# Reciprocals of the softmax moved to POOL in odd slots, and two more items of 36 turned by squares, in a top-k attention and GELU kernel

## The chip, the cores and the metric

The kernel runs on one core of a Trainium2 chip. The metric is the device time of one execution in microseconds, the median of several runs. The core's engines work side by side, each through its own instructions in order: PE (matmuls, and transposes as matmuls), DVE (searches for the largest values, block transposes), ACT (exponentials, GELU, copies out of PE's accumulators), POOL (small sums and products) and SP, which here issues DMAs. An instruction starts when those before it on its engine allow it and the semaphores it waits for have come.

## What is computed

```python
B, H, S, D = q.shape                      # 8, 8, 576, 64; top_k = 32
scores = scale * np.matmul(q, k.transpose(0, 1, 3, 2))
kth = np.partition(scores, -top_k, axis=-1)[..., -top_k:-top_k + 1]
scores = np.where(scores >= kth, scores, -1000000000.0)
scores = scores - np.max(scores, axis=-1, keepdims=True)
attn = np.exp(scores)
attn = attn / (np.sum(attn, axis=-1, keepdims=True) + 1e-09)
x = np.matmul(attn, v)                    # then (B,H,S,D) -> (B*S, H*D)
h = x @ w_in                              # 4608 x 512 times 512 x 2048
out = (0.5 * h * (1.0 + erf(h / sqrt(2)))) @ w_out
```

The division by the sum is what the change is about: each row of 576 exponentials is multiplied with 1 / (sum + 1e-9).

## The kernel before

The attention is cut into 144 items. An item is 128 query rows of two heads side by side, so its tile `s` has 128 partitions and 2 x 576 columns. 36 items (`RINGS`) belong to two batches and are called a ring here; slot or item m of 36 means its number modulo 36. The main loop goes over slots n = 0 to 147, and in slot n every stage works at an item of its own: PE makes the scores of item n+2, DVE searches item n, ACT selects and exponentiates item n-1, POOL normalises item n-1, item n-2 is turned, and the product with v is made for the pair of items that ends in n-3. The flag `few` is set from slot 13 on; the statements below that ask for it hold from there. Pieces of the MLP (`h_ps`, `y_ps`) are dealt out over the slots on PE, and what is left of them follows after the last search. The order of the instructions on each engine is the order in which this Python code issues them.

One slot, as far as the change touches it:

- DVE, `top_k` (L487): four rounds, each with two MAX8 (L513, one for each head), the first three with two MATCH_REPLACE8 behind (L516). The first two rounds go over 288 values each, the element-wise larger of the two halves of a row (`larger`, L442); the last two go over all 576. Between round two and three stands `middle()`, which is `square_p` of item n-2 (L610, the block transpose L614), if that item goes by squares. After the last MAX8 comes `last()`: in slots with `few` it issues `larger` of item n+2 and then `inverse` of item n-1, the reciprocal L534. `larger` is also called at the start of every slot for item n+1, where it does nothing if that has been done.
- POOL: `smaller` of item n+1 (L485), `add_small` of item n-1 (L540, adds 1e-9 to the sums), then, behind the search's end, `threshold` of item n (L527 the negative of the 32nd value, L528 the exponent's bias), `normalise` of item n-1 (L582, the product of the whole tile with the reciprocals), `sum_up` of item n+2 (L477), and small sums of the MLP's second matmul from a list.
- ACT: `select` of item n-1 (L547, waits for L527), and the exponential (L559), which leaves the sum of its row in `den`. Among these stand GELUs and copies out of the accumulators.
- An item is turned in one of two ways. By PE: nine transposes (L666 and eight of L680), which ACT copies to `pt` (L669, L695). Or by squares: DVE turns blocks of 32 x 32 in place, four DMAs write the tile to DRAM (`write_p`, L616) and four read it back into `pt` (`read_p`, L626), all on SP's queue. `squared` (L586) says which: from item 27 on most even items, the last items of a batch, and those odd ones for which `moved` holds.
- `moved(i)` (L596) holds for items 36 to 135 with i modulo 36 in `LATER`. A moved item's product with v is made one slot later than otherwise: in slot n, `mid = [n - 4]` is then attended in the middle of the slot, and only behind it is the next item's tile read. `room_in` (L1141) gives PE two MLP pieces more in the slot whose product is put off, and two fewer in the one before.

The tile `stat` holds, for each item and both heads, `neg`, `bias`, `den` and `rden`, two columns each. Of `s` there are seven buffers, of `lists` and `stat` two, of `pt` one.

Of the kernel before, what the change touches and what calls it, by code (L numbers as in the profile page):

```python
# [8 lines left out]
TOPK = 32  # L9
# [5 lines left out]
def kernel(  # L15
# [19 lines left out]
    nc = tc.nc  # L35
    f32, i32, u32 = mybir.dt.float32, mybir.dt.int32, mybir.dt.uint32
    bf16, i16, u16 = mybir.dt.bfloat16, mybir.dt.int16, mybir.dt.uint16
    AF = mybir.ActivationFunctionType
    ALU = mybir.AluOpType

    B, H, S, D = q.shape
    P = 128
# [19 lines left out]
    const = ctx.enter_context(tc.tile_pool(name="const", bufs=1))  # L62
# [47 lines left out]
    def flush():  # L110
        held[0] = False
        while late_issues:
            late_issues.pop(0)()
        late_issues.extend(later)
        later.clear()
# [61 lines left out]
    DIAGS = START - 1  # L177
    SINGLE = range(18, 28)
    words = {}
    bounds = const.tile([P, 2], f32, name="bounds")  # L180
    low, high = bounds[:, 0:1], bounds[:, 1:2]
    nc.gpsimd.memset(low, -EXP0 * 2.0**20)
    nc.gpsimd.memset(high, EXP0 * 2.0**-40)

# [85 lines left out]
    N = len(items)  # L272
# [4 lines left out]
    few = [False]  # L277
# [55 lines left out]
    S_of, stat_of = {}, {}  # L333
# [98 lines left out]
    def paired(i):  # L432

        return PAIRED <= i < N and i not in SINGLE
# [7 lines left out]
    def larger(i):  # L442

        if paired(i) and i not in have_larger:
            have_larger.add(i)
            nc.vector.tensor_tensor(lists_for(i)[:, :, 0], *halves_of(i), op=ALU.max)  # L446

    def into_of(i):

        if i < 2 and i not in into_lists:  # L450
            into_lists[i] = work.tile([P, 2, 2, HS], f32, tag="pt", bufs=1, name="into")
        return into_lists.get(i, lists_of[i])
# [28 lines left out]
    def smaller(i):  # L481

        if paired(i):
            both, top = lists_of[i][:, :, 1].bitcast(i32), lists_of[i][:, :, 0].bitcast(i32)
            nc.gpsimd.tensor_tensor(into_of(i)[:, :, 1].bitcast(i32), both, top, op=ALU.subtract)  # L485

    def top_k(i, last, middle):  # L487


        stat_of[i] = st = {  # L490
            "first": work.tile([P, 2, 8], f32, tag="first", name="first"),
        }
        stat = work.tile([P, 4, 2], f32, tag="stat", name="stat")
        st.update((n, stat[:, x]) for x, n in enumerate(("neg", "bias", "den", "rden")))
        top = work.tile([P, 2, 16], f32, tag="top", bufs=1, name="top")
        into = [st["first"]] + [
            top[:, :, 8:16] if r == TOPK // 8 - 1 else top[:, :, 0:8] for r in range(1, TOPK // 8)
        ]
        if paired(i):
            t = lists_of[i]  # L500
            u = into_of(i)
            both = u.rearrange("p e h n -> p e (h n)")
            rounds = [(t[:, :, 0], u[:, :, 0]), (u[:, :, 0], u[:, :, 0])]
            rounds = [(*(rounds[r] if 16 * r < TOPK else (both, both)), x) for r, x in enumerate(into)]
        else:
            s = S_of[i].rearrange("p (e n) -> p e n", e=2)
            t = work.tile([P, 2, S], f32, tag="lists", name="rest")
            rounds = [(s if r == 0 else t, t, x) for r, x in enumerate(into)]
        for r, (src, dst, x) in enumerate(rounds):
            if 16 * r == TOPK:  # L510
                middle()
            for e in range(2):
                nc.vector.max(x[:, e], src[:, e])  # L513
            if r < len(rounds) - 1:
                for e in range(2):
                    nc.vector.match_replace(dst[:, e], x[:, e], src[:, e], LOWEST)  # L516
            if r == len(rounds) - 1:
                last()

        st["kth"] = top[:, :, 15]  # L520

    def threshold(i):

        if i < 0 or i >= N:
            return
        st = stat_of[i]
        nc.gpsimd.tensor_scalar(st["neg"], st["kth"], -1.0, None, op0=ALU.mult)  # L527
        nc.gpsimd.tensor_tensor(st["bias"], st["kth"], st["first"][:, :, 0], op=ALU.subtract)  # L528

    def inverse(i):  # L530
        if i < 0 or i >= N:
            return
        st = stat_of[i]
        nc.vector.reciprocal(st["rden"], st["den"])  # L534

    def add_small(i):
        if i < 0 or i >= N:
            return
        st = stat_of[i]
        nc.gpsimd.tensor_scalar(st["den"], st["den"], 1e-9, None, op0=ALU.add)  # L540
# [50 lines left out]
            return i % RINGS != RINGS // 2 - 1  # L591
        return moved(i) or (i % 2 == 0 and i % RINGS != 12)

    LATER = (3, 13, 25, 31)

    def moved(i):  # L596

        return RINGS <= i < N - 8 and i % RINGS in LATER

# [7 lines left out]
    RINGS = 2 * len(items) // B  # L607
    turned = {}

    def square_p(i):  # L610

        if squared(i):
            s = S_of[i]
            nc.vector.transpose(s, s)  # L614

    def write_p(i):  # L616

        if squared(i):
            turned[i] = d = dram.tile([SQ, NJ + NM, P // SQ, P], f32, tag="turned", name="turned")
            s = S_of.pop(i).rearrange("p (x j) -> p x j", j=SQ)  # L620
            d = d.rearrange("i c k n -> i (c k) n")
            for a in range(P // SQ):
                rows = slice(a * SQ, (a + 1) * SQ)
                nc.sync.dma_start(out=d[:, :, rows], in_=s[rows])
# [498 lines left out]
    def mlp(n):  # L1123
        for _ in range(n):
            if done[0] >= len(pieces) or pieces[done[0]][0] > ready[0] or left[0] == 0:
                return
            pieces[done[0]][1]()
            done[0] += 1
            left[0] -= 1
            if eager[0]:  # L1130
                run_gelus()
                run_small(9)
# [72 lines left out]
    for n in range(ahead):  # L1205
# [87 lines left out]
        if few[0]:  # L1293
            room = ODD if n % 2 else 0
            if mid and (mid[0] in starts_next or mid[0] % RINGS == LATER[0]):
                mlp(1)
# [34 lines left out]
            softmax(n - 1, 1)  # L1331
        if n > 0:
            smaller(n + 1)
        add_small(n - 1)
        for piece in tr[-1:] + prep:
            piece(None)
            mlp(1)
# [6 lines left out]
        run_gelus()  # L1344
        if n < N:
            def last():
                if few[0]:
                    larger(n + 2)
                inverse(n - 1)

            top_k(n, last, lambda: square_p(n - 2))
            write_p(n - 2)
            flush()
            if n == 0:
                larger(1)
        else:
            inverse(n - 1)
        threshold(n)
        if n == 0:
            smaller(1)  # L1360
        normalise(n - 1)
# [59 lines left out]
```

## Time and profile before

| what | us |
|---|---|
| median of 3 runs | 1461.71 (1461.59 to 1461.82) |
| profiled execution | 1461.3 |
| its span on the core | 1459.5 |
| last search's end, from the span's start | 1375.3 |

The granted clock of PE was 1.0 over the run. Times in the lines below are microseconds from the span's start unless marked ns. In a timeline row the first number is the start, the second the duration (of a merged row the time from the first start to the last end), then engine, line and operation, what it writes and reads with sizes, how many, and in brackets how long the engine had been idle before it and what ended that. A row of a group has the busy time and the mean duration in ns, then the idle time just before such instructions. A row of the view of waits has the total wait, how often, and names the waiting instruction first and what it waited for behind the arrow. An instruction on DVE or POOL can start some 0.06 to 0.08 us before the one ahead of it ends, so costs are taken from start to start.

### The profile page before, as it was taken

How to read it: one execution, taken by the hardware profiler on the slowest of the kernel's cores; microseconds unless marked ns; L12 is line 12 of the kernel's file. 1: busy time of each engine (PE TensorE's matmuls, PEld its weight loads, DVE VectorE, ACT ScalarE, POOL GpSimd, SP SyncE). 2: the span in 40 equal slices, each digit the busy share in tenths (PEclk: the TensorE clock that was granted, in tenths of full speed). 3: DMA queues.
4: the chain of work that ended last, by engine and by line, in shares of the span. 5: the costliest groups of instructions: out<-in, count | busy, mean ns of one | idle time of the engine just before them, and what ended most of it. 6: DMA issues, size and time to landing. Idle time of an engine off the chain costs nothing.

```text
span 1459.5 us, 26550 instructions
## 1 busy us (share of the span) xinstructions
PE 1442.6 (99%) x8621; PEld 1123.9 (77%) x8621; DVE 1329.6 (91%) x3339; ACT 1056.4 (72%) x1883; POOL 1128.4 (77%) x1290
## 2 busy tenths in 40 slices
PE   8999999999999999999999999999999999999999
PEld 6776678877777777787777778787777777787887
DVE  7999999999999999999999999999999999999601
ACT  7999977777777777767777777777676767677620
POOL 6877657877798878878888878887788887878632
PEclk9999999999999999999999999999999999999999
DMA  7524310045454446456554365456554444543200
GB/s 196 150 87 126 84 48 1 9 98 104 90 113 89 87 87 142 82 113 128 111 99 96 65 117 116 90 112 127 117 102 106 90 80 84 127 98 85 53 15 15
DMA packets 591819, 136.49 MB, mean 94 GB/s; under 512 B 504352, under 2 KB 583232, under 8 KB 591680
## 3 DMA queue, kind: packets, MB, share of 16 engines
q1 hardware_dynamic: 590416, 134.37, 43.5%
q8 instruction: 68, 1.11, 0.3%
q14 instruction: 71, 0.58, 0.1%
q10 hardware_dynamic: 1200, 0.39, 0.1%
q0 software_dynamic: 64, 0.03, 0.0%
HBM read 85.19 MB, written 49.55 MB: 92 GB/s over the span
## 4 chain that ended last, share of the span: by engine, by line
PE 44%; POOL 11%; DVE 7%; issue 3%; ACT 3%; DMA 1%; SPq 0%; DVEq 0%; POOLq 0%; ACTq 0%
PE h_ps L820 17%; PE y_ps L976 11%; PE o L751 5%; PE s_ps L408 3%; POOL s L582 3%; DVE top L513 3%; DVE lists L516 2%; POOL lists L485 2%; POOL lists L477 2%; PE seven L974 2%; PE tp L680 2%; PE y_ps L938 2%; PE y_ps L941 1%; DMA turned<-s 1%; DVE s L614 1%
## 5 line engine op out<-in xcount | busy, mean ns | idle before, releaser
L820 PE MATMUL h_ps<-xT,w_in_sb 128*128 128x256 f32 (+1 forms) x2560 | 533.0, 361 | 0.0
L820 PEld LDWEIGHTS h_ps<-xT,w_in_sb 128*128 128x128 f32 x2560 | 438.9, 191 | 69.2 <-issue 10.9
L513 DVE MAX8 top<-lists 128x8 f32<-128x576 f32 (+1 forms) x792 | 475.9, 641 | 0.0
L547 ACT ACTIVATE s<-s,stat 128x576 f32<-128x576 f32 x288 | 219.2, 786 | 123.0 <-POOL stat L527 122.9
L516 DVE MATCH_REPLACE8 lists<-top,lists 128x288 f32<-128x288 f32 (+1 forms) x528 | 308.0, 589 | 0.0
L582 POOL TENSOR_TENSOR s<-s,stat 128x1152 f32<-128x1152 f32 x135 | 284.8, 2109 | 10.1 <-DVE stat L534 5.3
L559 ACT ACTIVATE s<-s,stat 128x576 f32<-128x576 f32 x288 | 225.2, 787 | 7.6
L485 POOL TENSOR_TENSOR lists<-lists 128x576 int32<-128x576 int32 x132 | 186.6, 1413 | 3.1
L477 POOL TENSOR_TENSOR lists<-s 128x576 int32<-128x576 int32 x133 | 188.2, 1415 | 0.0
L540 POOL TENSOR_SCALAR stat<-stat 128x2 f32<-128x2 f32 x144 | 44.4, 309 | 163.0 <-ACT s L559 156.1
L751 PE MATMUL o<-pt,raw_v 128*64 128x256 f32 x1280 | 152.9, 384 | 1.0 <-ACT pt L685 0.4
L416 ACT ACTIVATE s<-s_ps 128x1024 f32<-128x1024 f32 x127 | 126.4, 1046 | 35.2 <-PE s_ps L408 35.0
L751 PEld LDWEIGHTS o<-pt,raw_v 128*64 128x64 f32 x1280 | 86.8, 136 | 80.9 <-issue 38.1
L976 PE MATMUL y_ps<-w_out_sb,sum 128*128 128x256 f32 x472 | 140.4, 379 | 0.0
L408 PE MATMUL s_ps<-kt,qm 64*128 64x512 f32 x512 | 131.2, 621 | 1.1 <-ACT s L414 0.8
L836 ACT ACTIVATE g<-h_ps 128x512 f32<-128x512 f32 x144 | 78.2, 595 | 66.6 <-PE h_ps L820 66.0
L446 DVE TENSOR_TENSOR lists<-s 128x576 f32<-128x576 f32 x133 | 106.2, 799 | 17.8 <-ACT s L381 5.8
L976 PE MATMUL y_ps<-w_out_sb,g 128*128 128x256 f32 x480 | 116.4, 382 | 0.0
L516 DVE MATCH_REPLACE8 lists<-first,lists 128x288 f32<-128x288 f32 x264 | 114.4, 439 | 0.0
L513 DVE MAX8 first<-lists 128x8 f32<-128x288 f32 x268 | 105.8, 434 | 0.0
L976 PEld LDWEIGHTS y_ps<-w_out_sb,g 128*128 128x128 f32 x480 | 90.4, 190 | 15.0 <-issue 3.1
L976 PEld LDWEIGHTS y_ps<-w_out_sb,sum 128*128 128x128 f32 x472 | 89.8, 190 | 12.1
(162 smaller groups left out, 2359.0 us busy)
## 6 DMA issues: line engine op xcount, KB each, us to landing
turned<-s SPq DMA_DIRECT2D x272, 144.0 KB, 3.6
pt<-turned SPq DMA_DIRECT2D x272, 144.0 KB, 3.2
raw_v<-in_v_dram SPq DMA_DIRECT2D x64, 128.0 KB, 2.5
raw_q<-in_q_dram SPq DMA_DIRECT2D x112, 72.0 KB, 2.3
raw_k<-in_k_dram SPq DMA_DIRECT2D x112, 72.0 KB, 2.4
out_dram<-y SPq DMA_DIRECT2D x30, 256.0 KB, 3.1
w_out_sb<-in_moe_w_in_dram SPq DMA_DIRECT2D x14, 511.8 KB, 4.9
w_out_sb<-in_moe_w_out_dram SPq DMA_DIRECT2D x10, 511.8 KB, 4.1
```

The source lines that it names most:

```text
L408: nc.tensor.matmul(s_ps[:, e], lhsT=q_t[rows, :], rhs=kt[rows, main_keys(pair)], start=True, stop=True)
L416: nc.scalar.activation(spread(s, S + TL, SM), s_ps, func=AF.Copy, scale=scale)
L477: nc.gpsimd.tensor_tensor(t[:, :, 1].bitcast(i32), a.bitcast(i32), b.bitcast(i32), op=ALU.add)
L485: nc.gpsimd.tensor_tensor(into_of(i)[:, :, 1].bitcast(i32), both, top, op=ALU.subtract)
L513: nc.vector.max(x[:, e], src[:, e])
L516: nc.vector.match_replace(dst[:, e], x[:, e], src[:, e], LOWEST)
L547: nc.scalar.activation(s, s, func=AF.Prelu, bias=st["neg"][:, e : e + 1], scale=1.0, alpha=STEEP)
L559: nc.scalar.activation(s, s, func=AF.Exp, bias=st["bias"][:, e : e + 1], scale=1.0, accum_out=st["den"][:, e : e + 1],)
L582: nc.gpsimd.tensor_tensor(s, s, wide, op=ALU.mult)
L751: nc.tensor.matmul(o[e * D : (e + 1) * D, 0:n], lhsT=vt[:, j, e, :], rhs=pt[:, e * NJ + j if j < NM else NM, :], start=(j == 0), stop=(j = ...
L820: nc.tensor.matmul(h_tile(u)[:, i, :], lhsT=w_in_sb[:, ko, f * P : (f + 1) * P], rhs=xT[:, ko, c0 : c0 + n], start=(ko == 0), stop=(ko == ...
L976: nc.tensor.matmul(acc[names][:, k], lhsT=lhsT, rhs=rhs, start=(j == 0 and k == 0), stop=(j == FT // 2 - 1 and k == 1),)
```

## The change

Four things are done at once. A column of -1 is put beside the two bounds. In slots with `few` and odd n (`by_power`), `add_small` of item n-1 moves from before the transposes' tail to behind `threshold` of item n, and the reciprocal is made by POOL, as the sum to the power -1, right behind it; DVE's reciprocal falls away there. In even slots DVE keeps the reciprocal, but `larger` of item n+2 is no longer issued ahead of it, save in slot 34 of 36: it follows at the start of the next slot. In even slots with `few` the square of item n-2 is issued behind the two MAX8 of the third round and no longer ahead of them. And `LATER` has 5 and 23 as well: items 41, 59, 77, 95, 113 and 131 go by squares.

```diff
-    bounds = const.tile([P, 2], f32, name="bounds")
+    bounds = const.tile([P, 3], f32, name="bounds")
+    minus = bounds[:, 2:3]
...
+    nc.gpsimd.memset(minus, -1.0)
...
-            if 16 * r == TOPK:
+            if 16 * r == TOPK and not (few[0] and i % 2 == 0):
                 middle()
             for e in range(2):
                 nc.vector.max(x[:, e], src[:, e])
+            if 16 * r == TOPK and few[0] and i % 2 == 0:
+                middle()
...
+    def power(i):
+        st = stat_of[i]
+        nc.gpsimd.tensor_tensor(
+            st["rden"], st["den"],
+            bass.AP(tensor=minus.tensor, offset=minus.offset, ap=[list(minus.ap[0]), [0, 2]]),
+            op=ALU.pow,
+        )
...
-    LATER = (3, 13, 25, 31)
+    LATER = (3, 5, 13, 23, 25, 31)
...
-        add_small(n - 1)
+        by_power = few[0] and n % 2 and n < N
+        if not by_power:
+            add_small(n - 1)
...
             def last():
-                if few[0]:
+                if few[0] and n % RINGS == RINGS - 2:
                     larger(n + 2)
-                inverse(n - 1)
+                if not by_power:
+                    inverse(n - 1)
...
         threshold(n)
+        if by_power:
+            add_small(n - 1)
+            power(n - 1)
         if n == 0:
             smaller(1)
         normalise(n - 1)
```

## The prediction

> **What bounds the kernel now.** I read the busy times first, then the same by stage (one ring, 36 slots, from 704 to 1046 us, and what follows the last search), then who waited for whom, then the timeline around two kinds of slot.
>
> ```profile
> PE 1442.6 (99%) x8621; PEld 1123.9 (77%) x8621; DVE 1329.6 (91%) x3339; ACT 1056.4 (72%) x1883; POOL 1128.4 (77%) x1290
> ...
> 704.40:1046.40 342.00, 341.01 (x2014) 265.91 (x2013) 333.01 (x838) 249.08 (x450) 283.56 (x322) 1.00 0.52 105
> ...
> 1375.30:1459.50 84.20, 80.36 (x402) 68.66 (x399) 5.07 (x13) 18.20 (x39) 28.06 (x39) 0.99 0.04 13
> ```
>
> Columns of the last two: span, then busy us (instructions) of PE, its weight loads, DVE, ACT, POOL. In a ring DVE is idle 9.0 of 342.0 us and PE 1.0. Both look full, but PE's ends are modelled. The tail of 84.2 us is MLP work on PE alone, so a slot that gets longer before it moves the end by as much.
>
> The Trainium skill ("Trainium Kernel Development and Optimization", Performance Expectations) calls matmul busy time a bad metric and the share of weight loads a good one. By that share the ring (265.91 of 342.0, 78%) runs at 95% of the tail's rate (68.66 of 84.2, 82%), so that PE has some 16 us to spare in a ring; by the busy row 1.0. The first would leave more room for DVE to be the pace, the second less.
>
> ```profile
> POOL stat L540 <- ACT s L559: 156.1, 65, 5.7
> ACT s L547 <- POOL stat L527: 122.9, 45, 6.2
> ...
> DVE stat L534 <- POOL stat L540: 27.8, 27, 6.2
> ```
>
> Columns: total us, times, the longest. DVE's one large wait is the reciprocal behind POOL's add: 27.8 us in 27 of 144 slots, and that is the whole of what taking it away can give back on DVE. POOL waits 156.1 us for exponentials, ACT 122.9 us for thresholds. First, an ordinary pair, odd slot 75 and even slot 76:
>
> ```profile
> 730.83 1.41 DVE L513 MAX8 top<-lists 128x8 f32<-128x576 f32 x2
> 732.35 0.78 DVE L446 TENSOR_TENSOR lists<-s 128x576 f32<-128x576 f32 x1
> 733.04 0.15 DVE L534 RECIPROCAL stat<-stat 128x2 f32<-128x2 f32 x1
> 733.12 0.79 DVE L513 MAX8 first<-lists 128x8 f32<-128x288 f32 x2
> ...
> 740.29 1.40 DVE L513 MAX8 top<-lists 128x8 f32<-128x576 f32 x2
> 741.80 0.76 DVE L446 TENSOR_TENSOR lists<-s 128x576 f32<-128x576 f32 x1
> 742.48 0.15 DVE L534 RECIPROCAL stat<-stat 128x2 f32<-128x2 f32 x1
> 742.56 0.79 DVE L513 MAX8 first<-lists 128x8 f32<-128x288 f32 x2
> ```
> ```profile
> 731.43 0.22 POOL L540 TENSOR_SCALAR stat<-stat 128x2 f32<-128x2 f32 x1 [2.10 <-ACT s L559]
> 732.33 0.22 POOL L527 TENSOR_SCALAR stat<-top 128x2 f32<-128x2 f32 x1 [0.67 <-DMA raw_q<-in_q_dram]
> 732.50 0.67 POOL L528 TENSOR_TENSOR stat<-top,first 128x2 f32<-128x2 f32 x1
> 733.27 2.11 POOL L582 TENSOR_TENSOR s<-s,stat 128x1152 f32<-128x1152 f32 x1
> ...
> 740.27 1.41 POOL L485 TENSOR_TENSOR lists<-lists 128x576 int32<-128x576 int32 x1
> 741.76 0.22 POOL L540 TENSOR_SCALAR stat<-stat 128x2 f32<-128x2 f32 x1
> ```
>
> The searches end at 732.24 and 741.69; between one slot's end and the next first search DVE has 0.10 us of idle time, the larger-of-halves, and the reciprocal (0.08 from start to start). So DVE sets these slots. POOL has two halves that differ: from the even slot's end to the odd one's it waits (2.10 us ahead of the add at 731.43), but from 733.27 to the add at 741.76 it runs without a gap: normalise, sums, smaller halves. That add comes 0.07 us after the search's end, and today L446 hides it.
>
> Now a pair where DVE waits, slots 59 and 60:
>
> ```profile
> 578.90 1.41 DVE L513 MAX8 top<-lists 128x8 f32<-128x576 f32 x2
> 580.41 0.76 DVE L446 TENSOR_TENSOR lists<-s 128x576 f32<-128x576 f32 x1
> 582.19 0.17 DVE L534 RECIPROCAL stat<-stat 128x2 f32<-128x2 f32 x1 [1.02 <-POOL stat L540]
> 582.27 0.80 DVE L513 MAX8 first<-lists 128x8 f32<-128x288 f32 x2
> ...
> 591.90 0.80 DVE L513 MAX8 first<-lists 128x8 f32<-128x288 f32 x2
> ```
> ```profile
> 581.93 0.22 POOL L540 TENSOR_SCALAR stat<-stat 128x2 f32<-128x2 f32 x1 [2.53 <-ACT s L559]
> 582.23 0.22 POOL L527 TENSOR_SCALAR stat<-top 128x2 f32<-128x2 f32 x1
> 582.41 0.20 POOL L528 TENSOR_TENSOR stat<-top,first 128x2 f32<-128x2 f32 x1
> 582.56 2.11 POOL L582 TENSOR_TENSOR s<-s,stat 128x1152 f32<-128x1152 f32 x1
> ...
> 591.04 0.75 POOL L540 TENSOR_SCALAR stat<-stat 128x2 f32<-128x2 f32 x1
> ```
>
> **The change part by part.** *The power.* No row shows one on POOL. Nearest from below is a small operation on the same two columns, 0.22 us (L540 above); from above the 1152-column product, 2.11 us. I take 0.22, written P, since it has two columns like the first; a power takes more steps, so the range looks mostly upward. A page gives another cost: by the Trainium skill ("GPSIMD Engine Reference", Instruction dispatch) the first call of a freshly loaded kernel pays some 6 us without an instruction in the profile; no row here shows that, and by it the sum would be 6 us more, once.
>
> *An ordinary odd slot.* DVE loses the reciprocal: -0.08 us. On POOL the add, until now done in the idle half, moves behind the threshold pair, which ends at 733.17 (L528 takes 0.67 beside L446, against 0.20 at 582.41 away from it). Then the add to about 733.34, 0.08 of waiting for it, the power, 0.08 again: normalise starts at 733.49+P instead of 733.27. Behind it stands all of the gapless half, so the even slot's add ends not at 741.98 but at 742.20+P.
>
> *The even slot* now has the reciprocal ahead of L446 (slot 34 of 36 alone keeps the old order). It starts at 742.23+P, L446 0.08 later, the first search 0.68 after that: 742.99+P against 742.56. What L446 hid now stands open: +0.43+P a pair, 0.65 us. Queued behind the waiting reciprocal on DVE are L446 and the whole next search, and behind those the thresholds for which ACT already waits.
>
> *A late pair.* The wait of 1.02 us at 582.19 goes, with the reciprocal: the first search starts at 581.09, 1.18 earlier. But POOL's add at 581.93 waits for ACT, and power and normalise follow at 582.23 and 582.31+P, against 582.56: only 0.25-P sooner. So the next add ends near 591.01+P, and slot 60's reciprocal takes the wait: the search after it starts at 591.81+P against 591.90. The gain is handed back one slot later: -0.09+P.
>
> *Counted over a ring* in the third one's timeline: nine of 18 pairs have the even add from 0.07 to 0.71 us after the search's end (the last is below); where DVE waited already, what it waited is taken off, and the nine make +2.9+9P. Four are late ones, three with about -0.08+P and one with -0.8. In five the add is done long before; they gain about 0.1 each.
>
> ```profile
> 833.40 1.42 DVE L513 MAX8 top<-lists 128x8 f32<-128x576 f32 x2
> 834.91 1.14 DVE L446 TENSOR_TENSOR lists<-s 128x576 f32<-128x576 f32 x1
> ...
> 835.53 0.61 POOL L540 TENSOR_SCALAR stat<-stat 128x2 f32<-128x2 f32 x1
> ```
>
> *Items 5 and 23 of 36*, from item 36 to 135: six items go by squares. Each adds a square on DVE and eight DMAs on SP, and takes nine transposes from PE and two copies from ACT:
>
> ```profile
> L614 DVE STREAM_TRANSPOSE s<-s 128x1152 f32<-128x1152 f32 x68 | 92.8, 1365 | 0.0
> L680 PE MATMUL tp<-ident,s 128*128 128x128 f32 x536 | 69.6, 273 | 0.0
> L695 ACT COPY pt<-tp 128x1024 f32<-128x1024 f32 x65 | 66.3, 1020 | 34.9 <-PE tp L680 34.6
> turned<-s SPq DMA_DIRECT2D x272, 144.0 KB, 3.6
> pt<-turned SPq DMA_DIRECT2D x272, 144.0 KB, 3.2
> ```
>
> DVE: 6 x 1.29 (1365 ns less the usual overlap) = +7.7 us. PE: 69.6/536 = 0.13 us a transpose, nine of them 1.2, six items 7.0 less, worth nothing where DVE is the pace. The DMAs (6.8 us a round trip, DMA share 0.52) lie behind a whole slot, as those of the four items per ring that go this way already; the product waits one slot more, as theirs does. Without that cover an item would hold PE up to its 2.3 us of products.
>
> *Squares two searches later* cost no work. Their normalise has to be done: it now ends near 735.6+P, the square would start near 737.5, so up to P = 1.9 nothing waits. The write starts 1.3 us later, hidden as above.
>
> **The sum.** Three rings: 3 x (2.9+9P) = 14.6 at P = 0.22; late pairs -1.2; the five others -1.2; squares +7.7. Some of this falls into waits of DVE for others: 9.0 us idle in a ring, less 36 x 0.10 fixed, less 3.5 of the late waits already used, leaves 1.9, times three -5.7. Together +14.2. The slots before item 36, where most adds are late, I take as even. The profiled execution took 1461.3 us for its span of 1459.5, 0.4 below the median of the runs; 1461.3 + 14.2 gives 1475.5.
>
> **The rivals.** *PE sets the pace, and the kernel gets faster.* For it: PE is 99% busy and idle 1.0 us in a ring. DVE's new waits then fall into time that it has. The six items save 7.0, less perhaps 1 for switches: 1455. Against it: the ordinary slots, where DVE's rows stand end to end, and that PE is itself held by thresholds:
>
> ```profile
> 934.10 1.44 ACT L547 ACTIVATE s<-s,stat 128x576 f32<-128x576 f32 x2 [3.62 <-POOL stat L527]
> ...
> 938.26 0.49 PE L373 MATMUL tp_t<-kt,qm 128*128 128x128 f32 x2 [0.32 <-ACT p L995]
> ```
>
> ACT waits 3.62 us for a threshold, and PE for the copy that stands behind it. This decides if PE's work in a ring exceeds DVE's, 334 to 340 us after the change.
>
> *The power is dear.* P = 1 adds 12 x 0.78 a ring, 28 in all: 1504; the upper bound of 2.11 would add 68: 1543. It decides from P of about 0.5 on; for it, only that nothing shows a power.
>
> *The parts cancel.* The late waits gained are kept, because an earlier threshold lets exponentials and so the adds come earlier, some 3 us a ring, and PE gains some of its 7: 1461 to 1464. Against it, in slot 59 ACT is busy with slot 58's exponentials when the threshold would come.
>
> *The change doesn't do what it says:* the waits on DVE are not less but elsewhere; that is my forecast's own mechanism.
>
> **How the numbers follow.** Forecast (slower, 1465 to 1490) 0.52; dear power 0.12; PE as the pace 0.27; cancelling 0.09. About 0.2% is what can be told from no change (2.9 us). Faster 0.27, same 0.09, slower 0.64. The range is 1453 to 1492: it takes in most of PE's case and leaves out the dear power's upper part. The forecast's own range is 1465 to 1490.
>
> **What would show it.** Right: reciprocals in even slots with 0.3 to 1 us of idle time before them, released by L540's successor; normalise in odd slots 1.4 to 1.8 us after the search's end; ordinary pairs longer by 0.5 to 0.8; DVE's idle time in a ring about as large as now or larger. Wrong: PE's rows as dense as now with a ring under 341 us; even adds ahead of the search's end; a power over 0.5 us.

## The result and the profile after

The changed kernel takes 1499.35 us (median of 6 runs, 1498.71 to 1501.21) against 1461.76 (6 runs, 1461.52 to 1461.94): ratio 1.0259, 95% interval 1.0246 to 1.0272, so 37.6 us slower. The forecast was 1475.5, with a range up to 1492: the direction was right, and the size too small by 24 us.

The page of the changed kernel has these busy times and this summary of the chain of work that ended last; its line numbers are shifted (MAX8 is L515, `larger` L448, reciprocal L538, power L542, add L552, threshold L531 and bias L532, `normalise` L594, `smaller` L487, square L626, selection L559, exponential L571):

```profile
PE 1451.5 (97%) x8567; PEld 1117.1 (75%) x8567; DVE 1324.6 (88%) x3279; ACT 1050.6 (70%) x1871; POOL 1187.2 (79%) x1357
...
PE 24%; POOL 20%; DVE 20%; DMA 5%; issue 4%; ACT 3%; SPq 2%; DVEq 0%; POOLq 0%; ACTq 0%
```

On the page of the kernel before, the summary of that chain is:

```profile
PE 44%; POOL 11%; DVE 7%; issue 3%; ACT 3%; DMA 1%; SPq 0%; DVEq 0%; POOLq 0%; ACTq 0%
```

Less of the chain stands on PE, and more on POOL and DVE.

The same stages as before, from the view of windows (span, then busy us and instructions of PE, weight loads, DVE, ACT, POOL), the ring from the search's end in slot 72 to that in slot 108, and the tail behind the last search:

```profile
719.13:1073.23 354.10, 343.28 (x1998) 263.58 (x1997) 332.70 (x822) 247.16 (x446) 299.11 (x341) 1.00 0.54 108
1414.40:1498.20 83.80, 79.93 (x398) 68.15 (x396) 4.98 (x13) 18.18 (x39) 28.82 (x40) 1.00 0.04 13
```

A ring has grown from 342.0 to 354.1 us, while DVE's work in it is the same (332.7 us against 333.0) and POOL's has grown by 15.5. DVE's idle time is the difference: 21.4 us, before 9.0. The tail is as before. The view of waits names what DVE waits for:

```profile
ACT s L559 <- POOL stat L531: 194.6, 53, 7.4
POOL stat L531 <- DVE top L515: 171.3, 64, 5.1
DVE stat L538 <- POOL stat L552: 84.1, 61, 7.7
...
POOL stat L552 <- ACT s L571: 17.1, 13, 3.3
```

DVE's wait for the add has gone from 27.8 us to 84.1, although half of the reciprocals are gone. POOL's large wait has changed sides: before, 156.1 us for exponentials ahead of the add, now 171.3 us for searches ahead of the threshold. The power itself, in the view of groups and in the list of its instructions (the least, the median and the longest duration in ns, the first and the last start):

```profile
L542 POOL TENSOR_TENSOR stat<-stat,bounds 128x2 f32<-128x2 f32 x66 | 47.4, 719 | 5.5
```
```profile
L542 POOL TENSOR_TENSOR stat<-stat,bounds x66: 714/719/725, 131.5 to 1415.4; 128x2 f32<-128x2 f32 x66
```

P is 0.72 us, each time. An ordinary pair of slots, 76 and 77, in the timeline of DVE and of POOL:

```profile
755.91 1.41 DVE L515 MAX8 top<-lists 128x8 f32<-128x576 f32 x2
758.77 0.17 DVE L538 RECIPROCAL stat<-stat 128x2 f32<-128x2 f32 x1 [1.46 <-POOL stat L552]
758.86 0.76 DVE L448 TENSOR_TENSOR lists<-s 128x576 f32<-128x576 f32 x1
759.54 0.81 DVE L515 MAX8 first<-lists 128x8 f32<-128x288 f32 x2
...
766.72 1.40 DVE L515 MAX8 top<-lists 128x8 f32<-128x576 f32 x2
768.23 0.78 DVE L448 TENSOR_TENSOR lists<-s 128x576 f32<-128x576 f32 x1
768.93 0.81 DVE L515 MAX8 first<-lists 128x8 f32<-128x288 f32 x2
```
```profile
758.51 0.23 POOL L552 TENSOR_SCALAR stat<-stat 128x2 f32<-128x2 f32 x1
...
768.21 0.21 POOL L531 TENSOR_SCALAR stat<-top 128x2 f32<-128x2 f32 x1 [0.88 <-DVE top L515]
768.39 0.68 POOL L532 TENSOR_TENSOR stat<-top,first 128x2 f32<-128x2 f32 x1
769.15 0.22 POOL L552 TENSOR_SCALAR stat<-stat 128x2 f32<-128x2 f32 x1
769.45 0.72 POOL L542 TENSOR_TENSOR stat<-stat,bounds 128x2 f32<-128x2 f32 x1
770.25 2.10 POOL L594 TENSOR_TENSOR s<-s,stat 128x1152 f32<-128x1152 f32 x1
```

The even slot's search ends at 757.32. The add is over only at 758.74, the reciprocal has waited 1.46 us, and the next search starts 2.22 us after the end of the one before; before the change that was 0.87. In the odd slot (search's end 768.12) the threshold pair, the add and the power stand one behind the other, and `normalise` starts 2.13 us after the end. Before the change it was 1.03 (733.27 against 732.24), so everything in POOL's half that has no gap is 1.10 us later.

All slots of this ring, from their timelines, as sums of the time from one search's last MAX8 to the next search's first, against before: at the end of even slots +14.8 us, at the end of odd slots -5.6, and inside the searches +2.9 (two more squares of 1.29 make 2.6). Together 12.1, the growth of the ring.

### The profile page after: what moved, and what is told of

Read it like the earlier page. It is cut to its first block, busy times and chain, and to the rows that moved or that the text cites. A ratio compares the mean times of both kernels' runs of the same rounds, so it can differ in the third digit from the quotient of the medians.

```text
span 1498.2 us, 26668 instructions
## 1 busy us (share of the span) xinstructions
PE 1451.5 (97%) x8567; PEld 1117.1 (75%) x8567; DVE 1324.6 (88%) x3279; ACT 1050.6 (70%) x1871; POOL 1187.2 (79%) x1357
## 4 chain that ended last, share of the span: by engine, by line
PE 24%; POOL 20%; DVE 20%; DMA 5%; issue 4%; ACT 3%; SPq 2%; DVEq 0%; POOLq 0%; ACTq 0%
PE h_ps L832 9%; DVE top L515 8%; PE y_ps L988 6%; DVE lists L520 6%; POOL s L594 4%; PE o L763 3%; DMA turned<-s 3%; POOL lists L479 3%; POOL lists L487 3%; DVE s L626 2%; DVE first L515 2%; DVE lists L448 2%; PE s_ps L410 2%; POOL sum L870 1%; POOL sum L869 1%
## 5 line engine op out<-in xcount | busy, mean ns | idle before, releaser
L515 DVE MAX8 top<-lists 128x8 f32<-128x576 f32 (+1 forms) x792 | 476.4, 640 | 0.0
L559 ACT ACTIVATE s<-s,stat 128x576 f32<-128x576 f32 x288 | 217.9, 777 | 194.9 <-POOL stat L531 194.6
L594 POOL TENSOR_TENSOR s<-s,stat 128x1152 f32<-128x1152 f32 x135 | 285.7, 2117 | 5.5 <-DVE stat L538 0.3
L571 ACT ACTIVATE s<-s,stat 128x576 f32<-128x576 f32 x288 | 223.5, 778 | 7.8
L487 POOL TENSOR_TENSOR lists<-lists 128x576 int32<-128x576 int32 x132 | 185.8, 1408 | 3.1
L531 POOL TENSOR_SCALAR stat<-top 128x2 f32<-128x2 f32 x144 | 40.0, 278 | 186.6 <-DVE top L515 171.3
L448 DVE TENSOR_TENSOR lists<-s 128x576 f32<-128x576 f32 x133 | 103.6, 780 | 7.8 <-ACT s L383 1.0
L515 DVE MAX8 first<-lists 128x8 f32<-128x288 f32 x268 | 106.3, 435 | 0.0
L626 DVE STREAM_TRANSPOSE s<-s 128x1152 f32<-128x1152 f32 x74 | 100.4, 1356 | 0.0
```

Of the source, the lines that this page charges most:

```text
L559: nc.scalar.activation(s, s, func=AF.Prelu, bias=st["neg"][:, e : e + 1], scale=1.0, alpha=STEEP)
L571: nc.scalar.activation(s, s, func=AF.Exp, bias=st["bias"][:, e : e + 1], scale=1.0, accum_out=st["den"][:, e : e + 1],)
L594: nc.gpsimd.tensor_tensor(s, s, wide, op=ALU.mult)
```

## The experiments

| label | kernel | us, median (runs) | against before |
|---|---|---|---|
| e1_only_power | before, with the power alone | 1484.66 (1483.91 to 1486.74) | 1.0157 (1.0142 to 1.0172) |
| e2_only_order | before, with the even order alone | 1462.91 (1461.98 to 1463.60) | 1.0007 (0.9997 to 1.0016) |
| e3_only_items | before, with items 5 and 23 alone | 1468.22 (1467.85 to 1469.13) | 1.0043 (1.0028 to 1.0058) |
| e4_only_squares | before, with the later squares alone | 1463.93 (1463.62 to 1464.87) | 1.0014 (1.0005 to 1.0024) |
| e5_no_order | after, without the new order | 1493.17 (1491.54 to 1495.20) | 1.0216 (1.0199 to 1.0233) |
| e6_no_power | after, without the power | 1471.64 (1469.54 to 1473.10) | 1.0067 (1.0052 to 1.0082) |
| e7_no_items | after, without the two items | 1493.68 (1493.53 to 1493.87) | 1.0219 (1.0203 to 1.0234) |
| e8_no_squares | after, without the later squares | 1500.40 (1499.01 to 1501.82) | 1.0265 (1.0249 to 1.0280) |
| e9_mult | after, a product for the power | 1480.44 (1478.69 to 1481.42) | 1.0124 (1.0109 to 1.0139) |
| e10_twice | after, the power twice | 1540.97 (1540.88 to 1542.48) | 1.0542 (1.0526 to 1.0557) |
| e11_after_ahead | after, power ahead of the threshold | 1471.54 (1470.79 to 1472.48) | 1.0065 (1.0048 to 1.0082) |
| e12_power_ahead | before, power alone, ahead | 1466.52 (1464.98 to 1469.23) | 1.0032 (1.0021 to 1.0043) |
| f1_late_ahead | before, power ahead in six late slots | 1463.16 (1462.72 to 1464.58) | 1.0008 (0.9999 to 1.0017) |
| f2_late_behind | the same, behind the threshold | 1465.06 (1464.77 to 1465.80) | 1.0021 (1.0012 to 1.0030) |
| f3_late_more | f1 with five slots more | 1463.29 (1462.73 to 1463.89) | 1.0007 (0.9999 to 1.0016) |

The runs of before beside them had medians of 1461.72 (e1 to e4), 1461.92 (e5 to e8), 1462.13 (e9 to e12) and 1462.11 (f1 to f3).

### One part at a time

Each of the first four kernels has one part of the change, on the kernel before.

For the power (with `power`, and `add_small` and `inverse` under `by_power` as in the change), the order, the items and the squares:

```diff
+        by_power = few[0] and n % 2 and n < N
```
```diff
-                if few[0]:
+                if few[0] and (n % 2 or n % RINGS == RINGS - 2):
                     larger(n + 2)
```
```diff
-    LATER = (3, 13, 25, 31)
+    LATER = (3, 5, 13, 23, 25, 31)
```
```diff
-            if 16 * r == TOPK:
+            if 16 * r == TOPK and not (few[0] and i % 2 == 0):
                 middle()
...
+            if 16 * r == TOPK and few[0] and i % 2 == 0:
+                middle()
```

> Theory (POOL's gapless half: what is moved into it makes the even slot's add late, and DVE waits): the power measured 0.72 us, so with the add it makes the even add 1.02 us later; L446, still ahead of the reciprocal, hides about 0.8 of it. The late waits of odd slots go. Sum 1463 to 1469 us, and 0.3 to 0.6 us of DVE idle time before the reciprocals of ordinary even slots. Rival (the power's own time lies on the path): 66 x 0.72 = 47 us more, near 1509. Rival (DVE's late waits were the loss): 20 us less, near 1442.

> Reciprocal ahead of L446 in even slots, DVE making all reciprocals. Theory: where the add ends 0.3 to 0.9 us after the search, L446 no longer hides the wait: 0.1 to 0.3 us a pair, 1464 to 1470 us. Rival (PE or ACT sets the pace, so the order on DVE doesn't matter): 1461 to 1462.

> Items 5 and 23 of 36 by squares alone. Theory (DVE is the pace): six squares of 1.29 us less what falls into other waits, 1463 to 1470 us. Rival (PE is the pace): nine transposes less in six items, 1454 to 1457. Rival (the product made one slot later holds PE): over 1475.

> Squares behind the third round's MAX8 in even slots alone. Theory: the same work in another place, with a slot of time before pt is read: 1461 to 1463 us. Rival (the later DMAs hold the read of pt and so PE): over 1466.

By themselves the parts cost 22.9, 1.2, 6.5 and 2.2 us, 32.8 together, against 37.6 for the whole. The power is the largest by far. The items behave as the forecast's term for squares says (six squares, 7.7 us on DVE): a kernel in which PE set the pace would have become faster by them, so that rival falls here. What the order costs alone is not told apart from nothing by its interval; the later squares cost a little, for a reason that no run here shows.

The first run did not do what was expected of it. With `larger` still ahead of the reciprocal, the even slot was to be covered; it was 16 to 22 us slower than that. The end of its ordinary even slot 76 in the timeline, DVE and then POOL (here `larger` is L448, `smaller` L487, the reciprocal L536, the add L550):

```profile
752.74 1.41 DVE L515 MAX8 top<-lists 128x8 f32<-128x576 f32 x2
754.25 1.32 DVE L448 TENSOR_TENSOR lists<-s 128x576 f32<-128x576 f32 x1
755.70 0.17 DVE L536 RECIPROCAL stat<-stat 128x2 f32<-128x2 f32 x1
755.78 0.80 DVE L515 MAX8 first<-lists 128x8 f32<-128x288 f32 x2
```
```profile
753.56 1.40 POOL L487 TENSOR_TENSOR lists<-lists 128x576 int32<-128x576 int32 x1
755.05 0.61 POOL L550 TENSOR_SCALAR stat<-stat 128x2 f32<-128x2 f32 x1
```

There is hardly any idle time, and still the search starts 1.63 us after the last one's end. POOL's half is late by the power, so that its `smaller` now runs at the same time as DVE's `larger`, and `larger` takes 1.32 us instead of 0.76; the add behind it takes 0.61 instead of 0.22. Over the ring, `larger` alone (span and DVE's busy time on its line, in the view of windows, for the run with the power alone and for the kernel before):

```profile
715.84:1066.31 350.47, 34.90 (x36) 1.00 0.51 102
```
```profile
704.36:1046.39 342.03, 28.65 (x36) 1.00 0.52 105
```

This ring is 8.4 us longer: by the sums over its slots +9.1 at the end of even slots, +4.5 inside the searches and -5.1 at the end of odd slots. `larger` takes 6.25 us more, which shows as work, not as a wait, and 6.0 of that stand in the 9.1. In the whole execution its mean goes from 799 to 932 ns. The view of waits of this run has one more that before did not have:

```profile
DVE s L624 <- POOL s L592: 9.6, 29, 1.5
```

Squares wait for the later `normalise`, 29 of them 0.3 us on average; nine stand in this ring with 3.4 us, most of the 4.5 inside the searches. The forecast's room up to P = 1.9 was for squares that stand two searches (1.3 us) later; where they stood before, that leaves 0.6, less than the power takes.

### The whole without one part

Each undoes one hunk of the changed kernel: the order, the power (with the order that goes with it, so that `larger` stays ahead in odd slots), the items and the squares (these two back to the lines of before).

```diff
-                if few[0] and n % RINGS == RINGS - 2:
+                if few[0]:
                     larger(n + 2)
```
```diff
-        by_power = few[0] and n % 2 and n < N
+        by_power = False
```

> The changed kernel with the order of before: larger-of-halves ahead of the reciprocal in every slot; power, items and squares as changed. The run with the power alone showed its ordinary even slot's first search 1.6 us after the search's end where the changed kernel has 2.22, because there the larger-of-halves runs (stretched to 1.32 us beside POOL's smaller-of-halves) in the time in which the reciprocal waits. Theory A (the new order opens the wait that the old one covered in part): 0.6 us in some 9 pairs of 3 rings comes back, 16 us: 1483 (1479 to 1487). Rival B (the order matters as little as it did alone, +1.2): 1498 (1496 to 1500).

> The changed kernel with add and reciprocal of odd slots as before (DVE's reciprocal behind the larger-of-halves); even order, items and squares as changed. Theory A (all of the cost hangs on the power's place in POOL's gapless half): the other three, +1.2, +6.5 and +2.2 by themselves, add up: 1472 (1468 to 1475). Rival B (the order or the items cost by themselves what the single runs did not show): 1480 to 1490.

> The changed kernel with the four items per ring by squares as before, not six. Theory A (squares cost DVE, alone +6.5, and DVE sets the pace in both): 1493 (1490 to 1495). Rival B (with a longer ring DVE has idle time that takes the squares): 1498 to 1500. Rival C (PE's transposes, saved by the squares, would be in the way): 1501 to 1506.

> The changed kernel with the squares of even slots where they were. Theory A (in the changed order the even slot's search begins after the reciprocal and so after normalise could start; the square is then reached at much the same distance from normalise as before): 1499 (1496 to 1503). Rival B (the later normalise makes squares wait, as the power alone showed, 9.6 us in all): 1505 to 1510.

Without the power 1471.64: the three other parts cost 9.7 us together, as they do singly (9.9). With the power come 27.7. Without the items 5.7 are won, nearly what they cost alone: DVE has more idle time now, but the squares did not fall into it. The later squares make no difference that is told apart from nothing in the whole kernel (1500.40 against 1499.35, with overlapping runs): they remove the waits of squares, 6.6 us without them, and the wait for the add is 84.1 us with them and 76.3 without.

Going back to the old order gave 6.2 us, between what the two theories expected. Beside a late POOL, the old order holds `larger` up (983 ns on the mean in that run) and the new one leaves the reciprocal waiting; the second is dearer by 6 us with the power, and by 1 alone, which is not told apart from nothing.

### The length of the power

The product takes the place of the power on the same operands; the other kernel has the power twice. The kernel with the product leaves out a division: in an odd slot n the item at hand is n-1, so it is the even items that are not divided by their sums, and not the odd ones, as the expectation has it.

```diff
-            op=ALU.pow,
+            op=ALU.mult,
```
```diff
+        for _ in range(2):
...
+                op=ALU.pow,
```

> The changed kernel with a product (den times -1) where the power stood: same engine, place, operands and waits, another operation, so odd items are not divided by their sums. Theory A (the error was the duration of the power, 0.22 taken against 0.72): the product takes 0.2 to 0.25 us; twelve pairs a ring and three rings and a bit each get back 0.5 us, 18 to 23 us in all: 1479 (1474 to 1483). Rival B (the cost comes from place and order, whatever stands there): 1492 or more. Rival C (any operation of two tensors on these columns takes 0.7): 1499.

> The changed kernel with the power made twice, one behind the other, to the same place. Theory A (each microsecond in POOL's gapless half comes out at the end in some 12 of 18 pairs): 0.69 to 0.80 us more in 12 to 13 pairs of some 3.7 rings, 31 to 38 us: 1533 (1527 to 1540). Rival B (DVE's and ACT's waits take part of it, as a new slack forms elsewhere): 1505 to 1520.

The product's row in the view of groups, and its even slot 76 on DVE (search's end 749.97):

```profile
L542 POOL TENSOR_TENSOR stat<-stat,bounds 128x2 f32<-128x2 f32 x66 | 13.0, 197 | 5.5
```
```profile
750.91 0.17 DVE L538 RECIPROCAL stat<-stat 128x2 f32<-128x2 f32 x1 [0.95 <-POOL stat L552]
751.00 0.76 DVE L448 TENSOR_TENSOR lists<-s 128x576 f32<-128x576 f32 x1
751.68 0.81 DVE L515 MAX8 first<-lists 128x8 f32<-128x288 f32 x2
```

And the kernel with two powers, the two of an odd slot on POOL and the even slot 76 on DVE:

```profile
767.93 1.50 POOL L543 TENSOR_TENSOR stat<-stat,bounds 128x2 f32<-128x2 f32 x2
```
```profile
778.24 0.17 DVE L538 RECIPROCAL stat<-stat 128x2 f32<-128x2 f32 x1 [2.25 <-POOL stat L553]
```

In this slot the reciprocal waits 0.95, 1.46 and 2.25 us as the operation takes 0.20, 0.72 and 1.50: what is put into POOL's half comes out on DVE in full (0.51 for 0.52, 0.79 for 0.78). From the operation's start to that of `normalise` behind it the medians are 0.28 us for the product, 0.80 for one power. Over the whole, 0.52 us less in each of 66 slots make the kernel 18.9 us faster, 36 us for each us; 0.78 more make it 41.6 slower, 53 for each. The forecast's own slope was 12 pairs by 3 rings, 36. The steeper upper part says that nearly all pairs depend on it by then: the third ring grows by 6.0 us in the first step and by 13.1 in the second, which is 11.6 and 16.7 pairs of 18. That the lower slope is the forecast's 36 is in part luck: in the traces the three rings make 15.8 us of the first step, 30 for each us, and the slots before item 36, which the forecast had left out, 3.3.

### The place of the power

In the next two kernels (e11 and e12), add and power stand ahead of the odd slot's threshold, in the half in which POOL waited for exponentials before.

```diff
+        if by_power:
+            add_small(n - 1)
+            power(n - 1)
         threshold(n)
-        if by_power:
-            add_small(n - 1)
-            power(n - 1)
```

> The changed kernel with the add and the power of an odd slot ahead of its threshold pair instead of behind it. Theory A (it is the gapless half, from the threshold pair to the next add, that counts; ahead of the threshold POOL waits 2 us for ACT and the search): the power's cost mostly goes, +1.2, +6.5 and +2.2 of the other parts stay, and 0.2 us a pair by which the threshold may be later: 1474 (1468 to 1481). Rival B (thresholds made late by the power cost as much through ACT): 1490 to 1505.

> The kernel before, with the power alone (no other order, items or squares), add and power ahead of the odd slot's threshold. Theory A: ordinary odd slots lose 0.08 us of reciprocal and their normalise starts 0.2 later, which the larger-of-halves still hides; late pairs gain 1.0 in the odd slot and lose 0.8 in the even one: 1461 (1456 to 1466). Rival B (the later threshold delays ACT's exponentials and the next add): 1470 to 1485, as when the power stands behind the threshold.

The same instructions in this order take 27.8 us less, 1471.54. The odd slot 75 and the even slot 76 of the changed kernel with the power ahead, on POOL and on DVE (search ends 736.49 and 745.89):

```profile
735.12 0.22 POOL L552 TENSOR_SCALAR stat<-stat 128x2 f32<-128x2 f32 x1 [1.62 <-ACT s L571]
735.42 0.72 POOL L542 TENSOR_TENSOR stat<-stat,bounds 128x2 f32<-128x2 f32 x1
736.58 0.22 POOL L531 TENSOR_SCALAR stat<-top 128x2 f32<-128x2 f32 x1 [0.44 <-DVE top L515]
736.77 0.67 POOL L532 TENSOR_TENSOR stat<-top,first 128x2 f32<-128x2 f32 x1
737.39 2.10 POOL L594 TENSOR_TENSOR s<-s,stat 128x1152 f32<-128x1152 f32 x1
```
```profile
746.14 0.17 DVE L538 RECIPROCAL stat<-stat 128x2 f32<-128x2 f32 x1 [0.25 <-POOL stat L552]
```

The power is done before the search ends and POOL still waits 0.44 us for the search; `normalise` starts 0.90 us after the search's end instead of 2.13, and the reciprocal waits 0.25 instead of 1.46. The total is that of the kernel without the power, 1471.64: placed so, the power costs the changed kernel nothing that is told apart. Alone, on the kernel before, it costs 4.4 us there, just above the expected range. By the sums over the third ring's slots it loses 4.9 us at the end of even slots and 2.4 inside the searches, and wins 5.6 at the end of odd ones. Inside the searches squares wait for `normalise` (in the whole execution 3.5 us in nine) and MAX8 for the threshold pair, which has not yet read `top` (2.6 us in five).

### The late pairs

Left open after this was the step on pairs in which the reciprocal already waited: is the gain in the odd slot handed back in the next one? Here only six odd slots of a ring make the power, and the squares stand later behind three of them. In the second to fourth ring before the change, the reciprocal waits late in four of the six (15, 17, 19 and 23 of 36, by 0.6 to 1.0 us), not in 9 and 31.

```diff
+        by_power = few[0] and n % RINGS in (9, 15, 17, 19, 23, 31) and n < N
```

> The kernel before, with the power in six odd slots of a ring alone (9, 15, 17, 19, 23, 31 of 36, where the reciprocal waits late), add and power ahead of the threshold, and squares later only in even slots 18, 20, 24. Theory A (in the run with all odd slots ahead, these six gained 0.4 to 0.7 us a pair and the ordinary ones lost 0.1 to 0.9; a late wait that goes is kept in part): 3 us a ring less, 1453 (1450 to 1458). Rival B (my forecast's step: a late wait is handed back in the next slot): 1460 to 1463. Rival C (the later thresholds in these slots cost ACT more): 1464 to 1470.

> The same six slots, with add and power behind the threshold, as the change has them. By my forecast's step for late pairs (-0.09 + P each, P measured 0.72): six pairs of three rings at +0.63, 11 us: 1473. Theory A (the changed kernel's trace: what its late pairs won in the odd slot, 1.07 to 1.15, they lost in the even one, 1.16, though one or two won 0.4): 1462 (1459 to 1466).

> As the first of these, with five odd slots more (11, 27, 29, 33, 35 of 36), in which the run with all odd slots ahead gained the reciprocal's 0.07 us and lost nothing. Theory A: 0.35 us a ring less than the first, about 1 us: 1452 (1449 to 1457). Rival B (ACT or POOL takes it back): as the first or up to 3 us slower.

None is faster than before, so the theory that 3 us a ring are kept fell. In the third ring of the first of these (f1), the late pairs that begin with slots 87, 89, 91 and 95 change by -0.2, +0.8, 0.0 and 0.0 us: one keeps a little, two hand all of it back, and one loses. Slots 91 and 92 before (search's end of 91 at 884.55, of 92 at 895.02):

```profile
886.10 0.22 POOL L540 TENSOR_SCALAR stat<-stat 128x2 f32<-128x2 f32 x1 [3.62 <-ACT s L559]
...
895.21 0.75 POOL L540 TENSOR_SCALAR stat<-stat 128x2 f32<-128x2 f32 x1
```
```profile
886.43 0.80 DVE L513 MAX8 first<-lists 128x8 f32<-128x288 f32 x2
...
896.08 0.80 DVE L513 MAX8 first<-lists 128x8 f32<-128x288 f32 x2
```

The same with the power ahead in the late slots (search's end of 91 at 885.70, of 92 at 895.14):

```profile
886.70 0.22 POOL L552 TENSOR_SCALAR stat<-stat 128x2 f32<-128x2 f32 x1 [3.04 <-ACT s L571]
887.01 0.72 POOL L542 TENSOR_TENSOR stat<-stat,bounds 128x2 f32<-128x2 f32 x1
...
895.03 1.41 POOL L487 TENSOR_TENSOR lists<-lists 128x576 int32<-128x576 int32 x1
896.53 0.61 POOL L552 TENSOR_SCALAR stat<-stat 128x2 f32<-128x2 f32 x1
```
```profile
886.48 0.81 DVE L515 MAX8 first<-lists 128x8 f32<-128x288 f32 x2
...
895.25 1.81 DVE L448 TENSOR_TENSOR lists<-s 128x576 f32<-128x576 f32 x1
897.17 0.17 DVE L538 RECIPROCAL stat<-stat 128x2 f32<-128x2 f32 x1
897.25 0.80 DVE L515 MAX8 first<-lists 128x8 f32<-128x288 f32 x2
```

From the search's end in the odd slot to the next first MAX8: 1.88 before, 0.78 now, 1.10 won. From the even slot's end: 1.06 before, 2.11 now, 1.05 lost, all of it as a longer `larger` (1.81 us), behind which the reciprocal starts at once. The odd slot's add still waits for ACT: it comes 1.00 us after the search's end instead of 1.55, and the 0.72 of the power more than use that up, so that the even slot's add is 10.83 after it instead of 10.66. In slots 95 and 96 it is 1.18 won and 1.06 lost. The pair that loses, 89 and 90, does so inside the search of slot 90, where the second round's MAX8 waits until the threshold pair, now behind add and power, has read `top`, of which there is one buffer:

```profile
869.25 0.82 DVE L515 MAX8 top<-lists 128x8 f32<-128x288 f32 x2 [0.70 <-POOL stat L532]
```

Behind the threshold (f2) the total is 3.0 us above before, about a quarter of the 11 expected by the forecast's -0.09+P, a sum that counts all six slots as late. Of the 3.0, 1.8 stand before item 36. The third ring's four late pairs change by -0.5, +0.9, -0.1 and 0.0 us, 0.1 each on average, where -0.09+P would be 0.63.

## Why the prediction was wrong in size

- **What bounds the kernel: right for the ordinary slots.** After the change the pair is one closed cycle of POOL and DVE: from the odd search's end 2.13 us to `normalise`, 8.47 without a wait to the even add, 0.26 to the reciprocal, 0.77 to the first MAX8 and 8.58 of searching, 20.21 in all, as against 18.89 before.
- **The power: the step that failed.** The term P of the sum, the power's time on POOL, was mis-sized. I took P = 0.22, "since it has two columns like the first"; the runs show 0.72 (714 to 725 ns), between the bounds I had given; "a power over 0.5 us" was one of the prediction's own signs of being wrong. That a power takes more steps than such a small operation was an assumption there, and the product bears it out: with the same operands in the same place it takes 0.20 and gives 1480.4, within 5 us of the forecast. The length of the operation is worth 18.9 of the 24 us. The rival of a dear power, to which I gave 0.12 and for which "P of about 0.5" was the point, is what happened: the forecast's own terms at 0.72 give 1475.5 + 36 x 0.5 = 1493.5, above the range's upper end of 1492.
- **The first call.** The sentence on the Trainium skill ("GPSIMD Engine Reference", Instruction dispatch) would have made the sum 6 us more, once. No such time shows: the longest of 66 powers takes 725 ns, and the idle time ahead of all 66 is 5.5 us, 0.08 each.
- **Ordinary pairs: right in mechanism, short by 0.17.** Predicted +0.43+P a pair, with the measured P 1.15; measured 20.21 - 18.89 = 1.32. Nearly all of that is in the odd slot, where `normalise` was to start 1.97 us after the search's end and started 2.13 after it: I let the add follow the bias with 0.17 us to its end, and the row shows the usual 0.08 of waiting and 0.22 of work. "Ordinary pairs longer by 0.5 to 0.8" was for P = 0.22.
- **Late pairs: the handing back was right, its size was not.** Predicted -0.09+P, with the measured P +0.63; measured in the changed kernel -1.15 and +1.16 in slots 95 and 96, so nothing net, and -0.3 us for the third ring's four late pairs together. The add in slot 95 no longer waits for ACT, since the threshold pair stands ahead of it (search's end 945.74):

```profile
945.83 0.21 POOL L531 TENSOR_SCALAR stat<-top 128x2 f32<-128x2 f32 x1 [1.10 <-DVE top L515]
...
946.76 0.22 POOL L552 TENSOR_SCALAR stat<-stat 128x2 f32<-128x2 f32 x1
```

- **The six items: right.** 7.7 predicted on DVE; 6.5 alone, 5.7 in the whole.
- **The later squares: right in the whole.** At P = 0.72 no square waits in the changed kernel (without them 29 do, 0.2 us each), and what they cost is 2.2 alone and nothing that is told apart in the whole.
- **The absorption and the first slots: wrong.** 5.7 us were to fall into DVE's other waits, so that the three rings make 14.2. From the search's end in slot 36 to the last search's end they make 6.2, 6.1 and 6.7 with the product for the power, 19.0, which is 4.8 more. How much of that is missing absorption, and how much the ordinary pairs' 0.17 each less what the late pairs saved, is not told apart. In the changed kernel they make 34.8, against 32.2 by the forecast's terms at the measured P. And the slots before item 36, which I took as even, take 4.4 us more there (1.2 with the product). These 4.8 and 1.2, less 1.3 by which the part behind the last search is shorter with the product, are the rest of the 24 us beside the power's length.
- **PE as the pace, 0.27: it fell.** The two items alone made the kernel slower. In the ring PE's busy time went up from 341.0 to 343.3 us with 16 matmuls fewer, so it was not a measure of work. The share of weight loads, the number that the Trainium skill ("Trainium Kernel Development and Optimization", Performance Expectations) prefers, fell from 78% to 74% (263.58 of 354.10): the trace agrees with the page, as the busy time rose while the work fell.
- **The parts cancel, 0.09: it fell.** The 3 us a ring were not kept, ahead of the threshold or behind it: in the changed kernel, f1 and f2 only one of the four late pairs of the third ring, slots 87 and 88, keeps more than 0.1 us (0.2 to 0.5).

No version here beats the kernel before. The nearest, e2, f1 and f3, are 0.07% to 0.08% above it, with intervals that reach just below 1.

## What to carry to other kernels

Before an operation is moved to an engine "with idle time", find out in which half of that engine's cycle the idle time lies: the same add and power cost 27.8 us more behind the threshold than ahead of it, on an engine that was 77% busy. When an operation's cost is unknown and its slope is known (here about 36 us of total for each us), the forecast should lean on the range and not on the nearest row, because that one number carries most of the result. And a delay need not show as a wait: it can show as longer instructions of another engine, so compare the mean duration of the neighbours too.

## What the runs showed of the hardware

- The power of two tensors, 128 x 2 f32 on POOL, takes 719 ns, the product of the same two 197 ns. So 0.52 us are the operation's own and not the form's.
- DVE's element-wise larger of 128 x 576 takes 0.76 to 0.78 us beside POOL's two-column operations. Where POOL's integer `smaller` of the same size runs already, the larger ends 0.61 to 0.62 us after that one ends: with the power alone `smaller` ends at 754.96 and `larger` at 755.57, at the end of slot 92 of f1 at 896.44 and 897.06. The add behind `smaller` then ends just behind `larger` (755.66 and 897.14) and takes 0.61 instead of 0.22. The Trainium skill ("SBUF — State Buffer", SBUF: two separate sides) says that an operation of DVE with two inputs from SBUF and one of POOL that reads SBUF share a pair of ports as an exclusive lock, so that the later one waits for the whole of the earlier: these rows agree. The waiting shows as duration, not as idle time.
